# New places for the convolution's steps, the evacuations and the token sums beside the output projection of a fused convolution and SwiGLU kernel

## The chip, the cores and the metric

The kernel runs on one core of one Trainium2 chip. The metric is the device time of one execution in microseconds (us). Each core has a matrix engine (TensorE, PE in the profile, with its weight loads listed apart as PEld), a vector engine (VectorE, DVE), an activation engine (ScalarE, ACT), a general engine (GpSimd, POOL) and a queue that issues most DMAs here (SyncE, SP). Every engine works through its own queue in the order in which the program issued the instructions to it. An instruction whose input is not ready holds up everything behind it on that engine.

## The reference

`x` is 8 x 4096 x 192 in fp32. A causal depthwise convolution with seven taps comes first; each of eight heads of 24 channels has its own softmax-normalised taps. Its output is read as 32768 tokens of 192 channels. Each token is RMS-normalised and goes through a SwiGLU layer without bias.

```python
xn = x / rms * rms_g
g = xn @ w_gate                       # 192 -> 1536
silu = g * (1.0 / (1.0 + np.exp(-g)))
val = xn @ w_val                      # 192 -> 1536
return (silu * val @ w_out)           # 1536 -> 192
```

Everything is computed in fp32.

## The kernel before

**Tiling.** The tokens are cut into 32 pairs (`PAIRS`) of two tiles of 512 tokens. The gate half of the 192 to 1536 product lies in partitions 0 to 63 (`h = 0`), the value half in partitions 64 to 127 (`h = 1`). TensorE works on both halves beside each other. The `h = 1` stream runs `LAG = 138` planned units behind `h = 0`.

**A pair has two stages on TensorE.** In the first, four units (`NU`, function `unit`) each make three of the twelve 128-column blocks of the gate and the value product for both tiles. A bilinear scheme uses 15 matrix products where 18 would be needed, so sums of PSUM banks follow on the other engines; they are listed in `PLAN` (line 88). A code letter names the engine (`T` TensorE, `A` ScalarE, `V` VectorE, `G` GpSimd), a second the act (`P` product, `S` and `F` copies, `R` and `D` sums, `G` silu, `M` the gating multiply). The plan of a unit spans 1509 units but its last entries lie behind that, up to 1912: the last unit's tail falls into the second stage. In it are, on VectorE, four entries at 31, 102, 174 and 245 units after the second stage's start, on ScalarE two silus at 62 and 200, and on GpSimd three multiplies at 82, 243 and 403.

In the second stage (`outer`) TensorE multiplies the gated blocks by `w_out`: for two tiles `g` and four groups `j` of 128 tokens, twelve matmuls of 192 columns for each half. The two halves are sums over different parts of the contraction and are added when they leave PSUM: `low` (line 607) copies the `h = 0` bank by ScalarE, `upp` (line 611) adds the `h = 1` bank by VectorE, and `store` sends the tile out through SP.

**PSUM banks.** Each half has four banks (`free`, line 448). Tile `g = 0` uses all four, one for each `j`. Tile `g = 1` puts two `j` into one bank and so needs two banks; the first is the one that `low` and `upp` of `g = 0, j = 0` give back. The matmul that takes it is number `n = 48` of its half.

**What runs beside `outer`.** The convolution of the pair after next (`conv(p + 2, 1)`): tap 0 is eight `tensor_scalar` on VectorE (line 340, called the first tap below), taps 1 to 6 are eight multiplies each on ScalarE (line 355) and one addition of 128 x 1536 on VectorE (line 359). A multiply's result lies in one of three buffers (`prods`). The last step of `conv` issues the load of a later pair's `x` on SP. Then `norm(p + 2)`: eight squares with sums on ScalarE (line 371), two small instructions on GpSimd, eight scalings, half on ScalarE and half on VectorE. Further `fetch(p + 1)`, the four DMAs that bring the next pair's transposed tokens into `xb`, and `x_sums(p + 1)`: eleven sums of 128 x 512 on VectorE (line 441), which the bilinear scheme's products read in the next pair.

**Order.** Nothing is scheduled at run time. Every instruction, or every step of a generator between two `yield`s, is put on one list with a due time in planned units (`put`, `later`), and `emit` issues the list in the order of those times. The due time thus sets only the order in each engine's queue. For `outer`, `STEP` is 37.5 units a matmul, `OUT` is 3600 units for the stage, and `OVER` is how long after the last matmul of a group its evacuation is put. `base` in the code below is the start of `outer`.

Of the kernel before, what the change touches and what calls it, by code (L numbers as in the profile page):

```python
# [18 lines left out]
def kernel(  # L19
# [14 lines left out]
    H, K = weight.shape  # L34
# [31 lines left out]
    XSUM = (  # L66
        (0, 1, 4), (1, 2, 6), (2, 0, 6), (9, 3, 5), (3, 3, 8), (4, 7, 15), (5, 4, 15), (6, 5, 7),
        (7, 0, 1), (8, 1, 2), (9, 8, 15),
    )
# [71 lines left out]
    def load(p):  # L141

        if p >= PAIRS:
            return
        b, t0 = p // NB, (p % NB) * PT
        t = x_sb[p] = xs.tile([P, NJ + HALO, D], F32, name="x_sb")
        first = 0
        if t0 == 0:


            nc.vector.memset(t[0:1, 0:HALO, :], 0.0)
            nc.sync.dma_start(
                out=t[0:1, HALO:, :], in_=x[b, 0:NJ, :].rearrange("(o r) d -> o r d", o=1)
            )
            parts = ((1, 16), (16, P))
        else:
            parts = ((0, P),)
        for lo, hi in parts:
            row = x[b, t0 + lo * NJ - HALO, :]
            src = bass.AP(  # L160
                tensor=row.tensor, offset=row.offset,
                ap=[[NJ * D, hi - lo], [D, NJ + HALO], [1, D]],
            )
            nc.sync.dma_start(out=t[lo:hi, :, :], in_=src)
# [161 lines left out]
    def conv(p, alone=0):  # L326


        if p >= PAIRS:
            return  # L330
        t = x_sb.pop(p)
        y = ys[p] = work.tile([P, NJ, D], F32, name="y")
        for k in range(K):
            xk = t[:, k : k + NJ, :]
            if k < alone:
                for h in range(H):
                    hs = slice(h * GS, (h + 1) * GS)
                    w = taps[:, h, k : k + 1]
                    if k == 0:
                        nc.vector.tensor_scalar(  # L340
                            out=y[:, :, hs], in0=xk[:, :, hs], scalar1=w, scalar2=None,
                            op0=ALU.mult,
                        )
                    else:
                        nc.vector.scalar_tensor_tensor(
                            out=y[:, :, hs], in0=xk[:, :, hs], scalar=w, in1=y[:, :, hs],
                            op0=ALU.mult, op1=ALU.add,
                        )
                    if h % 4 == 3:
                        yield  # L350
                continue
            m = y if k == 0 else prods.tile([P, NJ, D], F32, name="m")
            for h in range(H):
                hs = slice(h * GS, (h + 1) * GS)
                nc.scalar.mul(m[:, :, hs], xk[:, :, hs], taps[:, h, k : k + 1])  # L355
                if h % 2:
                    yield
            if k > 0:
                nc.vector.tensor_tensor(out=y[:], in0=y[:], in1=m[:], op=ALU.add)  # L359
            yield  # L360
        load(p + 1)

    def norm(p, fast=False, share=False):
        if p >= PAIRS:
            return
        y = ys[p]
        ss = work.tile([P, NJ], F32, name="ss")
        sq = work.tile([P, D], F32, name="sq")
        na = NJ // 2 if fast else NJ
        for j in range(na):  # L370
            nc.scalar.activation(  # L371
                out=sq[:], in_=y[:, j, :], func=AF.Square, accum_out=ss[:, j : j + 1]
            )
            if j % 2:
                yield
        if fast:
            s2 = prods.tile([P, NJ, D], F32, name="m")
            nc.vector.tensor_tensor(
                out=s2[:, na:, :], in0=y[:, na:, :], in1=y[:, na:, :], op=ALU.mult
            )  # L380
            nc.vector.tensor_reduce(out=ss[:, na:], in_=s2[:, na:, :], axis=AX.X, op=ALU.add)
        r = work.tile([P, NJ], F32, name="r")
        nc.gpsimd.tensor_scalar(  # L383
            out=r[:], in0=ss[:], scalar1=1.0 / D, scalar2=1e-6, op0=ALU.mult, op1=ALU.add
        )
        nc.gpsimd.tensor_tensor(out=r[:], in0=r[:], in1=nhalf[:], op=ALU.pow)
        yield
        for j in range(NJ):
            if (fast or share) and j % 2:
                nc.vector.tensor_scalar(  # L390
                    out=y[:, j, :], in0=y[:, j, :], scalar1=r[:, j : j + 1],
                    scalar2=None, op0=ALU.mult,
                )
            else:
                nc.scalar.mul(y[:, j, :], y[:, j, :], r[:, j : j + 1])
            if j % 2:
                yield

    def place(p):

        if p >= PAIRS:
            return
        y = ys.pop(p)
        nt = work.tile([P, D // Q, Q, NJ], F32, name="nt")
        yv = y[:].rearrange("p j (c a) -> p c j a", a=Q)
        nv = nt[:].rearrange("p c b j -> p c j b")
        for c in range(D // Q):  # L410
            nc.vector.transpose(out=nv[:, c], in_=yv[:, c])
            yield
        xd = scr[p] = dram.tile([D, PT], F32, name="xd")
        to = xd[:].rearrange("(c a) (q t) -> q a c t", a=Q, q=NQ)
        for q in range(NQ):
            nc.sync.dma_start(
                out=to[q], in_=nt[q * Q : (q + 1) * Q].rearrange("p c b j -> p c (b j)")
            )
        yield

    def x_op(i):
        return xb[:, i // KP, i % KP, :] if i < 2 * KP else xc[:, i - 2 * KP, :]
# [13 lines left out]
    def x_sums(p):  # L436
        if p >= PAIRS:
            return

        for d, a, b in XSUM:  # L440
            nc.vector.tensor_tensor(out=xc[:, d, :], in0=x_op(a), in1=x_op(b), op=ALU.add)  # L441
            yield
# [18 lines left out]
    def put(at, do):  # L461
        heapq.heappush(line, (at, next(tick), do))

    def emit(until):
        while line and line[0][0] < until:
            heapq.heappop(line)[2]()
# [108 lines left out]

    STEP = 100 * D / T
    OUT = 2 * (T // P) * FC * STEP
    OVER = 120

    def outer(p, hts, base):  # L580

# [48 lines left out]
        def evac(dst, bks, w):  # L630
            put(base + n * STEP + OVER, functools.partial(low, dst, bks, w))
            put(base + n * STEP + LAG + OVER, functools.partial(upp, dst, bks, w))

        for g in range(2):
# [9 lines left out]
            else:  # L644
                for j in range(0, 4, 2):
# [3 lines left out]
                    evac(o_sb[:, j : j + 2, :].rearrange("p j d -> p (j d)"), b, 2 * D)  # L649
            put(base + n * STEP + LAG + OVER + 1, functools.partial(store, g, o_sb))  # L650

# [67 lines left out]
    def later(it, *places):  # L719
        for at in places:  # L720
            put(at, functools.partial(next, it, None))
# [3 lines left out]
    for p in range(PAIRS):  # L725
        base = p * PAIR
        if p > 0:
            hts = []
            pl = place(p + 1)
            for u in range(NU):  # L730
                at = base + u * SPAN
                put(at - 1, lambda u=u, hts=hts, at=at: hts.append(unit(u, at)))
                later(pl, *[at + i for i in ROOM])
        base += NU * SPAN

        def begin(p=p, hts=hts, base=base):
            outer(p, hts, base)

        put(base - 1, begin)
        put(base + LAG, functools.partial(fetch, p + 1))  # L740
        if p == 0:
            later(ws, *range(int(base), int(base) + 600, 100))
        cv = conv(p + 2, 1)
        later(cv, base + 40, base + 100, *[base + 290 + 66 * i for i in range(15)],
              *[base + 1390 + 66 * i for i in range(16)])
        later(norm(p + 2, share=True), *[base + 2400 + 128 * i for i in range(4)],
              *[base + 2920 + 90 * i for i in range(6)])
        later(x_sums(p + 1), *[base + 1680 + 150 * i for i in range(len(XSUM) + 1)])
        emit(base + OUT)
    emit(float("inf"))  # L750
# [28 lines left out]
```

## Time and profile before

| what | value |
|---|---|
| median of 3 runs | 2859.8 us (2857.16 to 2860.85) |
| the profiled execution's own time | 2857.99 us |
| its span, first to last instruction | 2856.2 us |
| mean granted TensorE clock | 0.989 |
| PE busy | 2734.8 us, 96% |
| PEld busy | 1872.4 us, 66% |
| DVE busy | 2282.2 us, 80% |
| ACT busy | 2199.9 us, 77% |
| POOL busy | 1206.7 us, 42% |

Shares are averages over both stages of all pairs. The prediction looks into single pairs. It uses the list of waits, the chain of waits that ended last, timelines of one engine, and tables of windows; each is explained where it is quoted. All times in those views are microseconds from the span's start.

### The profile page before, as it was taken

The numbers are of one execution on the slowest core, as the hardware profiler recorded it, in microseconds if no ns is written. First come the engines' busy times: TensorE is split into PE (matmuls) and PEld (weight loads), VectorE is DVE, ScalarE is ACT, GpSimd is POOL, SyncE is SP. The second block draws the span as 40 slices with busy tenths as digits, with TensorE's granted clock in tenths as the row PEclk, the third lists the DMA queues.
The fourth block names the chain that finished last, engine by engine and source line by source line (L and its number), as shares of the span: only waits on it lengthen the run. The fifth ranks groups of instructions, "written<-read, shape, count | busy, mean of one in ns | idle before, by whom it ended". The sixth has DMA issues, their size and how long they took to land.

```text
span 2856.2 us, 53815 instructions
## 1 busy us (share of the span) xinstructions
PE 2734.8 (96%) x20144; PEld 1872.4 (66%) x20144; DVE 2282.2 (80%) x3631; ACT 2199.9 (77%) x5013; POOL 1206.7 (42%) x1033
## 2 busy tenths in 40 slices
PE   3999999999999999999999999999999999999999
PEld 1576776666676667766667766677666677666776
DVE  7788878887778888788887888887888878888864
ACT  6678778877778787788777787877887777878754
POOL 1854334443334543344433345433444333454333
PEclk9999999999999999999999999999999999999999
DMA  6221222112121211221121212112211222121110
GB/s 155 70 64 43 53 65 59 39 44 63 53 65 39 59 44 53 65 59 40 42 64 54 65 39 59 43 54 64 59 40 42 65 54 64 39 60 43 34 45 12
DMA packets 95606, 155.24 MB, mean 54 GB/s; under 512 B 6896, under 2 KB 64752, under 8 KB 91256
## 3 DMA queue, kind: packets, MB, share of 16 engines
q1 hardware_dynamic: 94272, 150.20, 20.7%
q8 instruction: 158, 2.59, 0.4%
q0 software_dynamic: 512, 1.57, 0.2%
q14 instruction: 104, 0.85, 0.1%
q10 hardware_dynamic: 560, 0.03, 0.0%
HBM read 101.44 MB, written 50.33 MB: 53 GB/s over the span
## 4 chain that ended last, share of the span: by engine, by line
PE 75%; ACT 12%; DVE 8%; issue 3%; POOL 0%; DMA 0%; DVEq 0%; SPq 0%; POOLq 0%
PE ps L508 53%; PE ps L587 20%; ACT m L355 11%; DVE y L340 3%; DVE tile L530 2%; PE ps L558 1%; DVE ht L530 1%; DVE xc L441 1%; DVE ps L519 1%; ACT tile L534 0%; DVE o_sb L611 0%; POOL wf L301 0%; ACT o_sb L607 0%; DMA xb<-xd 0%; PE ps L598 0%
## 5 line engine op out<-in xcount | busy, mean ns | idle before, releaser
L508 PE MATMUL ps<-xc,wf 64*128 64x512 f32 x4960 | 1540.5, 593 | 0.0
L587 PE MATMUL ps<-wo_sb,ht 64*128 64x192 f32 x12288 | 1103.6, 329 | 65.3 <-DVE o_sb L611 52.2
L587 PEld LDWEIGHTS ps<-wo_sb,ht 64*128 64x128 f32 x12288 | 1082.9, 191 | 96.8 <-DVE o_sb L611 60.8
L508 PEld LDWEIGHTS ps<-xc,wf 64*128 64x128 f32 x4960 | 697.0, 187 | 559.1 <-issue 413.8
L537 POOL TENSOR_TENSOR ht<-ht,tile 128x512 f32<-128x512 f32 x620 | 773.7, 1272 | 651.0 <-ACT tile L534 551.0
L508 PE MATMUL ps<-xb,wf 64*128 64x512 f32 x2480 | 1038.4, 589 | 0.0
L517 ACT ACTIVATE tile<-ps 128x512 f32<-128x512 f32 x1488 | 820.1, 597 | 166.2 <-PE ps L508 136.4
L508 PEld LDWEIGHTS ps<-xb,wf 64*128 64x128 f32 x2480 | 419.2, 187 | 233.3 <-issue 202.4
L355 ACT ACTIVATE m<-x_sb,taps 128x192 f32<-128x192 f32 x1520 | 543.2, 444 | 7.0 <-DMA x_sb<-in_x_dram 6.3
L534 ACT ACTIVATE tile<-tile 128x512 f32<-128x512 f32 x620 | 374.8, 625 | 128.0 <-DVE tile L530 124.2
L359 DVE TENSOR_TENSOR y<-y,m 128x1536 f32<-128x1536 f32 x190 | 334.9, 1763 | 166.6 <-ACT m L355 166.0
L530 DVE TENSOR_TENSOR tile<-ps,tile 128x512 f32<-128x512 f32 x620 | 411.6, 680 | 0.0
L525 POOL TENSOR_TENSOR tile<-tile,tile 128x512 f32<-128x512 f32 x248 | 310.4, 1274 | 233.0 <-DVE tile L521 233.0
L530 DVE TENSOR_TENSOR ht<-ps,tile 128x512 f32<-128x512 f32 x620 | 401.3, 680 | 0.0
L383 POOL TENSOR_SCALAR r<-ss 128x8 f32<-128x8 f32 x32 | 6.6, 207 | 690.6 <-ACT sq L371 663.5
L530 DVE TENSOR_TENSOR ps<-ps,tile 128x512 f32<-128x512 f32 x248 | 173.5, 699 | 148.3 <-PE ps L508 146.4
L517 ACT ACTIVATE ps<-ps 128x512 f32<-128x512 f32 x372 | 216.2, 581 | 46.8 <-PE ps L508 32.1
L611 DVE TENSOR_TENSOR o_sb<-ps,o_sb 128x192 f32<-128x192 f32 (+1 forms) x192 | 78.1, 420 | 178.6 <-PE ps L508 94.2
L521 DVE COPY tile<-ps 128x512 f32<-128x512 f32 x248 | 170.1, 686 | 5.9 <-PE ps L508 5.8
L371 ACT ACTIVATE sq<-y 128x192 f32<-128x192 f32 x252 | 91.5, 363 | 102.4 <-DVE y L359 95.5
L519 DVE TENSOR_SCALAR ps<-ps 128x512 f32<-128x512 f32 x248 | 164.2, 695 | 0.0
L607 ACT COPY o_sb<-ps 128x192 f32<-128x192 f32 (+1 forms) x192 | 68.7, 358 | 111.3 <-PE ps L587 111.3
(54 smaller groups left out, 1206.1 us busy)
## 6 DMA issues: line engine op xcount, KB each, us to landing
xb<-xd SPq DMA_DIRECT2D x128, 384.0 KB, 6.3
x_sb<-in_x_dram SPq DMA_DIRECT2D x24, 1344.0 KB, 6.5
xd<-nt SPq DMA_DIRECT2D x128, 192.0 KB, 3.4
out_dram<-o_sb SPq DMA_DIRECT2D x64, 384.0 KB, 2.8
x_sb<-in_x_dram SPq DMA_DIRECT2D x8, 1176.0 KB, 9.4
ht<-in_moe_w_gate_dram SPq DMA_DIRECT2D x12, 192.0 KB, 9.0
ht<-in_moe_w_val_dram SPq DMA_DIRECT2D x12, 192.0 KB, 7.3
o_sb<-in_moe_w_out_dram POOLq DMA_DIRECT2D x8, 192.0 KB, 2.8
```

The source lines that it names most:

```text
L355: nc.scalar.mul(m[:, :, hs], xk[:, :, hs], taps[:, h, k : k + 1])
L359: nc.vector.tensor_tensor(out=y[:], in0=y[:], in1=m[:], op=ALU.add)
L371: nc.scalar.activation(out=sq[:], in_=y[:, j, :], func=AF.Square, accum_out=ss[:, j : j + 1])
L508: nc.tensor.matmul(out=new(v, h, True) if first else old(v, h), lhsT=wf[u][HALF[h], WAT[i], :], rhs=x_op(XOP[i])[HALF[h]], start=first, st ...
L517: nc.scalar.activation(out=dst, in_=src, func=AF.Copy, scale=float(s))
L519: e.tensor_scalar(out=dst, in0=src, scalar1=-1.0, scalar2=None, op0=ALU.mult)
L521: e.tensor_copy(out=dst, in_=src)
L525: e.tensor_tensor(out=grab((v, h)), in0=a, in1=b, op=plus(s))
L530: e.tensor_tensor(out=dst, in0=src, in1=t, op=plus(s))
L534: nc.scalar.activation(out=dst, in_=src, func=AF.Silu)
L537: e.tensor_tensor(out=hv(v), in0=src, in1=tl["g", v][:], op=ALU.mult)
L587: nc.tensor.matmul(out=bank(h, bks[h])[:, w : w + D], lhsT=hts[f // NF][HALF[h], g, f % NF, j * P : (j + 1) * P], rhs=wo_sb[HALF[h], f, :] ...
```

## The change

`OVER` goes from 120 to 50: all evacuations, and the stores behind them, are put 70 units earlier.

The first tap's two steps of four instructions move from 40 and 100 units after the start of `outer` to 250 and 255, behind the last unit's four VectorE entries (31, 102, 174, 245).

The ScalarE multiplies of tap 1 to 6 start at 280, 612, 944, 1276, 1668 and 2000, two every 83 units, with the VectorE addition 332 units after each start. Before, they came two every 66 units from 290 on, with a gap from 1214 to 1390, and the additions were at 554, 884, 1214, 1654, 1984 and 2314. The `x` load's issue goes from 2380 to 2340.

`norm`: the four steps of squares go from 2400, 2528, 2656, 2784 to 2560, 2688, 2816, 2944; the GpSimd step from 2920 to 3070; the four steps of scalings from 3010, 3100, 3190, 3280 to 3340, 3380, 3420, 3460.

`x_sums`: before, one every 150 units from 1680 to 3180. Now at 1690, 2020, 2060, and then one every 70 units from 2345 to 2835.

No instruction is added, removed or changed in its operands. `PLAN` is untouched.

```diff
-    OVER = 120
+    OVER = 50
...
-        cv = conv(p + 2, 1)
-        later(cv, base + 40, base + 100, *[base + 290 + 66 * i for i in range(15)],
-              *[base + 1390 + 66 * i for i in range(16)])
-        later(norm(p + 2, share=True), *[base + 2400 + 128 * i for i in range(4)],
-              *[base + 2920 + 90 * i for i in range(6)])
-        later(x_sums(p + 1), *[base + 1680 + 150 * i for i in range(len(XSUM) + 1)])
+        starts = [280 + 332 * k + (60 if k > 3 else 0) for k in range(K - 1)]
+        later(conv(p + 2, 1), *[base + i for i in (250, 255)],
+              *[base + i + 83 * n for i in starts for n in range(5)], base + 2340)
+        later(norm(p + 2, share=True), *[base + 2560 + 128 * i for i in range(4)],
+              base + 3070, *[base + 3340 + 40 * i for i in range(5)])
+        later(x_sums(p + 1), *[base + i for i in (1690, 2020, 2060)],
+              *[base + 2345 + 70 * i for i in range(len(XSUM) - 2)])
```

## The prediction

> **What bounds the kernel now.** First, what TensorE waits for. In the list of waits, restricted to TensorE, a row is: the waiting line, who released it, us in total, times, longest.
>
> ```profile
> PE ps L587 <- DVE o_sb L611: 52.2, 29, 1.8
> PE ps L587 <- ACT o_sb L607: 13.0, 29, 0.7
> ```
>
> Both wait 29 times, once a pair in 29 of the 32, on an evacuation of `outer`. Second, the chain of waits: start, length, what. The rows are like pieces of several pairs.
>
> ```profile
> 154.78 48.31 PE ps L508 x223
> ...
> 2336.84 48.31 PE ps L508 x216
> ...
> 2407.08 11.11 PE ps L587 x133
> 2423.17 48.31 PE ps L508 x216
> ...
> 2511.17 48.31 PE ps L508 x216
> ...
> 2581.41 12.79 PE ps L587 x133
> 2599.18 48.31 PE ps L508 x216
> ...
> 2669.42 11.11 PE ps L587 x133
> 2685.51 50.52 PE ps L508 x226
> ...
> 2768.74 50.52 PE ps L508 x226
> ```
>
> From the first product stage shown to the one at 2599.18 there are 28 pairs in 2444.40 us, 87.30 us each. There are two kinds: 2423.17 - 2336.84 = 86.33 us, with 133 matmuls in 11.11 us, and 2511.17 - 2423.17 = 88.00, where a like piece (2581.41) takes 12.79. The last pair shown takes 2768.74 - 2685.51 = 83.23 us: it has no convolution beside `outer` and no such wait. So **a pair without the waits is 83.23 us**, the short kind loses 3.10, the long kind 4.77. The two idle gaps in the list of waits come to only 65.2/29 = 2.25 a pair, because the other half's stream is still draining when one half stops.
>
> Third, windows of 3 to 36 us: the stretch, its length, busy time of PE, PEld, DVE, ACT, POOL (with counts), granted clock, DMA share, GB/s. The first is `outer` of the first pair, the second that of a pair of the long kind, the third and fourth the stall in it and the part after.
>
> ```profile
> 122.00:153.30 31.30, 31.30 (x382) 31.30 (x381) 23.43 (x35) 23.68 (x74) 17.06 (x23) 1.00 0.28 83
> 640.16:676.30 36.14, 33.90 (x385) 33.31 (x383) 26.05 (x39) 24.61 (x77) 5.64 (x5) 0.95 0.35 94
> 656.40:659.80 3.40, 1.56 (x14) 1.27 (x14) 2.44 (x3) 3.40 (x13) 0.00 (x0) 1.00 0.00 0
> 661.04:664.45 3.41, 3.41 (x26) 3.41 (x24) 3.41 (x6) 2.46 (x8) 0.00 (x0) 0.50 0.02 5
> ```
>
> In the long kind the clock stands at 0.50 for 3.41 us right after the stall, and half of that, 1.7 us, is the 1.67 us between the kinds. In the first pair TensorE is busy for the whole 31.30 us, though that pair has all of the convolution beside it.
>
> **Why the evacuation is late.** Timelines around one `outer`, TensorE, then VectorE, then ScalarE: start, length, engine, line, count, idle time before it and who ended it. A row of several instructions spans them all.
>
> ```profile
> 640.16 0.32 PE L587 MATMUL ps<-wo_sb,ht 64*128 64x192 f32 x1
> 656.68 1.56 PE L587 MATMUL ps<-wo_sb,ht 64*128 64x192 f32 x14 [0.44 <-ACT o_sb L607]
> 660.04 0.43 PE L587 MATMUL ps<-wo_sb,ht 64*128 64x192 f32 x2 [1.80 <-DVE o_sb L611]
> ...
> 641.14 3.66 DVE L340 TENSOR_SCALAR y<-x_sb,taps 128x192 f32<-128x192 f32 x8
> 657.36 1.76 DVE L359 TENSOR_TENSOR y<-y,m 128x1536 f32<-128x1536 f32 x1 [1.22 <-ACT m L355]
> 659.04 0.68 DVE L441 TENSOR_TENSOR xc<-xb 128x512 f32<-128x512 f32 x1
> 659.64 0.35 DVE L611 TENSOR_TENSOR o_sb<-ps,o_sb 128x192 f32<-128x192 f32 x1
> ...
> 645.43 0.63 ACT L534 ACTIVATE tile<-tile 128x512 f32<-128x512 f32 x1 [4.23 <-DVE tile L530]
> 645.97 10.46 ACT L355 ACTIVATE m<-x_sb,taps 128x192 f32<-128x192 f32 x30
> ```
>
> Call the stage's start b, here 640.16. The first tap goes first on VectorE (641.14). The last unit's sum stands behind it, so ScalarE's last silu waits 4.23 us and starts at b + 5.27; the multiplies queued behind it start at b + 5.81. Thirty of them end at 656.43, and only then comes `low`, which releases TensorE's first stall. VectorE's fourth addition waits for two more multiplies, one token sum follows, and `upp` runs at 659.64 (b + 19.48); TensorE goes on at 660.04. One cause lies behind both stalls: 3.6 us of lateness handed from VectorE to ScalarE and back.
>
> **The sums ahead of the first tap.** The trace has this order already, in the last pairs, where the first tap is missing. TensorE, VectorE, ScalarE:
>
> ```profile
> 2735.86 0.32 PE L587 MATMUL ps<-wo_sb,ht 64*128 64x192 f32 x1
> ...
> 2736.84 0.68 DVE L530 TENSOR_TENSOR tile<-ps,tile 128x512 f32<-128x512 f32 x1
> 2738.04 0.68 DVE L530 TENSOR_TENSOR ht<-ps,tile 128x512 f32<-128x512 f32 x1
> ...
> 2737.56 0.63 ACT L534 ACTIVATE tile<-tile 128x512 f32<-128x512 f32 x1 [0.66 <-DVE tile L530]
> 2748.77 0.32 ACT L607 COPY o_sb<-ps 128x192 f32<-128x192 f32 x1 [10.58 <-PE ps L587]
> ```
>
> The sum starts at b + 0.98, the silu at b + 1.70. The multiplies follow a silu by 645.97 - 645.43 = 0.54, so at **b + 2.24 instead of 5.81**. Thirty take 10.46: b + 12.70. In the last row `low` waits for nothing but TensorE, and starts at b + 12.91. So ScalarE is there 0.2 us early and `low` runs when the matmuls allow it. One silu, at b + 1.70, is the only ScalarE work that gains from VectorE directly; all the rest is the queue moving up.
>
> **The first tap behind them** starts 0.60 (half of the distance 2738.04 - 2736.84, two sums) after the last sum, at b + 2.78. What it takes there no row shows. Its median row, its neighbour on GpSimd in the pair above, and the rows of the first pair, which has b = 121.94:
>
> ```profile
> L340 DVE TENSOR_SCALAR y<-x_sb,taps x248: 303/308/1327, 11.0 to 2653.9; 128x192 f32<-128x192 f32 x124
> ...
> 640.79 2.52 POOL L537 TENSOR_TENSOR ht<-ht,tile 128x512 f32<-128x512 f32 x2 [1.11 <-ACT tile L534]
> ...
> 121.94 0.65 PE L587 MATMUL ps<-wo_sb,ht 64*128 64x192 f32 x3
> 134.86 0.32 ACT L607 COPY o_sb<-ps 128x192 f32<-128x192 f32 x1 [1.76 <-PE ps L587]
> 135.91 1.76 DVE L359 TENSOR_TENSOR y<-y,m 128x1536 f32<-128x1536 f32 x1 [3.09 <-ACT m L355]
> 138.29 0.34 DVE L611 TENSOR_TENSOR o_sb<-ps,o_sb 128x192 f32<-128x192 f32 x1
> 145.20 0.36 ACT L371 ACTIVATE sq<-y 128x192 f32<-128x192 f32 x1 [3.13 <-DVE y L359]
> 151.13 1.49 ACT L395 ACTIVATE y<-y,r 128x192 f32<-128x192 f32 x4 [1.70 <-POOL r L386]
> ```
>
> At the median 308 ns, eight take at most 2.5 us; here they took 3.66, beside two multiplies of 1.26 each on GpSimd. In the new place a third such multiply comes up beside them. I bound the step by 2.5 and 3.66 + 1.26 = 4.92, and take 3.66, the same instructions beside the same engine. Even at 4.92 it ends at b + 7.70. Three additions, 1.68 from start to start (659.04 - 657.36), then start at 7.70, 9.38 and 11.06; the third also needs 24 multiplies, b + 2.24 + 24 x 0.349 = 10.61. The fourth tap's multiplies reuse the first one's buffer from 10.61 on, and the first addition ends at 7.70 + 1.76 = 9.46. So VectorE is free at b + 12.74 at the latest. [...]
>
> **Evacuations 70 units earlier, multiplies and additions to match.** In the new order ScalarE has `low` (1512.5) ahead of the fourth tap's last two multiplies (1525); VectorE has the fourth addition (1608), then `upp` (1650.5), and the first token sum (1690) behind it instead of ahead. In the first pair, `low` was followed by the same two multiplies, and the fourth addition started 135.91 - 134.86 = 1.05 after it. So here: `low` b + 12.91, addition b + 13.96, `upp` b + 15.64 to 15.98. That is the added head-of-line wait: ScalarE can now stand at `low` for TensorE (0.2 us), with multiplies behind it. When is `upp` too late? In the first pair it ended at 138.63, b + 16.69, and TensorE never idled. **So `upp` has at least 0.7 us to spare** where it was 3.1 us late against the same mark (659.99 - 640.16 = 19.83, less 16.69). `low` ran at b + 12.92 in that pair, as it will here. The other three pairs of evacuations stand between multiplies and additions as before, and the banks they free are wanted only 24 matmuls later.
>
> **Squares, scalings, token sums, the loads and stores.** They cost what they did. Ahead of the squares stand the sixth addition and, on ScalarE, the same multiplies and copies; in the first pair they started 145.20 - 134.86 = 10.34 after `low` and the scalings 5.93 after that. That gives b + 23.25, 29.18 and, with 1.49, an end at 30.67. What each must not hold up:
>
> ```profile
> 667.04 1.28 DVE L441 TENSOR_TENSOR xc<-xb,xc 128x512 f32<-128x512 f32 x2
> ...
> 2767.49 0.48 ACT L607 COPY o_sb<-ps 128x384 f32<-128x384 f32 x1 [7.55 <-PE ps L587]
> ```
>
> The last `low` is ready at 2767.49 - 2735.86 = b + 31.63, 1.0 later. The eight token sums behind the sixth addition take some 0.6 each (two in 1.28) and end at 23.25 + 8 x 0.6 = b + 28.1; the next products come after the 31.3 us of the first window. SP's queue keeps its order (fetch, store, load, store), each a little earlier, and none of its transfers appears in TensorE's waits after the start-up. I cost all of these at nothing; without the 1.0 us of cover each further us would cost 29, one in each pair.
>
> **The sum.** Nothing late is left on TensorE's side, so each of 29 pairs falls to 83.23 us. 28 pairs give 2444.40 - 28 x 83.23 = 113.96. The 29th (2669.42) is of the short kind, 3.10. Together **117.1 us**: 29 x 3.10 = 89.9 for the stalls, and 27.2, some 16 stretches of 1.67, for the clock. From the profiled execution's 2857.99 that leaves 2740.9. The median of the runs, 2859.8, stands 1.8 above that execution; I say **2742**.
>
> **The rivals.**
>
> *A short stall stays (0.09).* My chain has 0.7 us to spare at `upp` and rests on ScalarE reaching `low` at b + 12.70. If multiplies, port or buffers cost 0.9 us more than that, `upp` ends at b + 16.7, and each half us beyond costs 14.5: 2756 at half a us. For it: 0.2 us of room on ScalarE is thin. Against: every duration is from the same instructions.
>
> *The half clock stays (0.04).* Free of stalls, 16 stretches of 1.67 could remain: 2741 + 27 = 2768. [...] Against: neither the first pair nor the last two show a loss; at 16 in 29 by chance, three such pairs in a row have (13/29)^3, 9%. [...]
>
> *The change doesn't do what it says (0.02).* If the sums were late by their own inputs, not by the first tap, nothing moves: 2858. The row at 2736.84 speaks against it.
>
> *Slower (0.03).* The tail spills into the next pair: eight sums and the scalings now stand packed behind the sixth addition, and the scalings ahead of the last `low` and the next pair's bank copies. With over 1.0 us of delay there TensorE waits, at 29 us for each us; the gain is used up at 1.0 + 117.1/29 = 5.0, and at 6 the time is 2741 + 5 x 29 = 2886. For it: the squares are placed 160 units later than before. Against: in the first pair the squares had 3.13 us of idle ahead of them, so the additions set their time, not their place.
>
> **How the numbers follow.** The forecast has 0.82: all stalls go. It and the short stalls up to half a us make the range: 2736 (the runs before lie 2.6 below their median; three more for the bounds of the first tap and rounding) to 2757. A measurement of this kernel can tell about 0.2%, 5.7 us, from no change. Forecast, short stall and half clock are faster: 0.95; same 0.02; slower 0.03.
>
> **What would show it.** In the changed profile: TensorE's two waits on line 607 and 611 gone or under 0.2 us a pair; clock 1.000 but for the start-up; the silu about b + 1.7, multiplies b + 2.2, `low` b + 12.9 ended by TensorE, `upp` b + 15.6; pairs of 83.2 us throughout. I am wrong if `low` is still preceded by a multiply without idle time, if `upp` is behind b + 16.7, or if a wait on a token sum or a bank copy appears at the start of the product stage.

## The result and the profile after

The changed kernel takes 2741.43 us (median of 4 runs, 2740.69 to 2743.35), the kernel before 2860.1 us in the same comparison (median of 4, 2857.16 to 2860.85). The ratio is 0.9588, 95% interval 0.9571 to 0.9605. The forecast was 2742 us, within 2736 to 2757.

First, the chain of work that ended last, by engine, on the page of the kernel before and then of the changed kernel:

```profile
PE 75%; ACT 12%; DVE 8%; issue 3%; POOL 0%; DMA 0%; DVEq 0%; SPq 0%; POOLq 0%
```

```profile
PE 97%; POOL 1%; DVE 0%; DMA 0%; issue 0%; ACT 0%; SPq 0%; POOLq 0%; DVEq 0%
```

TensorE's own work is now nearly the whole chain; ScalarE and VectorE had 20% of it before.

The list of what TensorE waited for, changed kernel, whole (us in total, times, longest):

```profile
PE ps L558 <- DMA xb<-xd: 45.0, 1, 45.0
PE ps L558 <- ACT tile L564: 3.5, 1, 3.5
PE ps L558 <- DVE wf L271: 2.1, 1, 2.1
PE ps L558 <- DVE ht L565: 0.3, 1, 0.3
```

All four are at line 558, the first pair's products at the start-up. The waits on lines 607 and 611 are gone. A window over one `outer` of the changed kernel (length, then busy time of PE, PEld, DVE, ACT, POOL, clock, DMA share, GB/s):

```profile
621.49:652.90 31.41, 31.41 (x386) 31.41 (x384) 25.45 (x39) 24.67 (x76) 6.04 (x5) 1.00 0.41 109
```

TensorE is busy for all of 31.41 us. In the kernel before, the pair shown needed 36.14 us for the same matmuls. The timeline of this pair, TensorE, VectorE, ScalarE, answers to the rows that the prediction showed; its b is 621.49:

```profile
621.49 0.65 PE L587 MATMUL ps<-wo_sb,ht 64*128 64x192 f32 x3
...
622.38 0.68 DVE L530 TENSOR_TENSOR tile<-ps,tile 128x512 f32<-128x512 f32 x1
...
624.17 3.09 DVE L340 TENSOR_SCALAR y<-x_sb,taps 128x192 f32<-128x192 f32 x8
...
635.41 1.76 DVE L359 TENSOR_TENSOR y<-y,m 128x1536 f32<-128x1536 f32 x1 [1.61 <-ACT m L355]
637.09 0.35 DVE L611 TENSOR_TENSOR o_sb<-ps,o_sb 128x192 f32<-128x192 f32 x1
...
623.09 0.63 ACT L534 ACTIVATE tile<-tile 128x512 f32<-128x512 f32 x1 [0.67 <-DVE tile L530]
623.62 10.46 ACT L355 ACTIVATE m<-x_sb,taps 128x192 f32<-128x192 f32 x30
634.36 0.32 ACT L607 COPY o_sb<-ps 128x192 f32<-128x192 f32 x1 [0.28 <-PE ps L587]
...
643.62 0.36 ACT L371 ACTIVATE sq<-y 128x192 f32<-128x192 f32 x1 [1.93 <-DVE y L359]
...
650.22 1.49 ACT L395 ACTIVATE y<-y,r 128x192 f32<-128x192 f32 x4 [2.50 <-POOL r L386]
653.11 0.48 ACT L607 COPY o_sb<-ps 128x384 f32<-128x384 f32 x1 [1.39 <-PE ps L587]
```

The sum comes at b + 0.89, the silu at 1.60, the multiplies at 2.13, `low` at 12.87, ended by TensorE, the fourth addition at 13.92, `upp` at 15.60. Both `low` rows now end their idle time on TensorE: ScalarE waits for the matmuls and not the other way round.

Counted from the trace's matmul records, `outer` (first matmul to the first product of the next pair) takes 31.42 us in every one of the 31 pairs that have a next one. Before, it took 31.42 in the first and in the last of these, about 34.5 in 13 and about 36.2 in 16. The product stage takes 51.81 us in both, with a few that are up to 0.16 us longer.

### The profile page after: what moved, and what is told of

The parts are those of the page before. It is cut to its first block, busy times and chain, and to the rows that moved or that the text cites. A ratio compares the mean times of both kernels' runs of the same rounds, so it can differ in the third digit from the quotient of the medians.

```text
span 2739.5 us, 53838 instructions
## 1 busy us (share of the span) xinstructions
PE 2684.4 (98%) x20144; PEld 2168.9 (79%) x20144; DVE 2277.5 (83%) x3631; ACT 2206.7 (81%) x5013; POOL 1226.2 (45%) x1033
## 4 chain that ended last, share of the span: by engine, by line
PE 97%; POOL 1%; DVE 0%; DMA 0%; issue 0%; ACT 0%; SPq 0%; POOLq 0%; DVEq 0%
PE ps L508 58%; PE ps L587 37%; PE ps L558 2%; PE ps L598 0%; POOL wf L301 0%; DMA xb<-xd 0%; DMA xd<-nt 0%; DVE nt L411 0%; DVE wf L271 0%; ACT y L395 0%; DVE ht L565 0%; POOL o_sb L205 0%; POOL r L386 0%; DVE y L359 0%; POOL wf L297 0%
## 5 line engine op out<-in xcount | busy, mean ns | idle before, releaser
L508 PE MATMUL ps<-xc,wf 64*128 64x512 f32 x4960 | 1510.4, 593 | 0.0
L508 PEld LDWEIGHTS ps<-xc,wf 64*128 64x128 f32 x4960 | 808.6, 187 | 314.2 <-ACT ps L517 40.4
L587 PE MATMUL ps<-wo_sb,ht 64*128 64x192 f32 x12288 | 1048.1, 323 | 0.0
L587 PEld LDWEIGHTS ps<-wo_sb,ht 64*128 64x128 f32 x12288 | 1044.4, 187 | 0.8 <-issue 0.4
L508 PE MATMUL ps<-xb,wf 64*128 64x512 f32 x2480 | 1008.2, 589 | 0.0
L508 PEld LDWEIGHTS ps<-xb,wf 64*128 64x128 f32 x2480 | 444.8, 187 | 161.8 <-DVE ps L519 0.9
L525 POOL TENSOR_TENSOR tile<-tile,tile 128x512 f32<-128x512 f32 x248 | 310.7, 1276 | 212.7 <-DVE tile L521 212.7
L383 POOL TENSOR_SCALAR r<-ss 128x8 f32<-128x8 f32 x32 | 28.1, 879 | 677.7 <-ACT sq L371 650.8
```

What stands on the lines that cost most here:

```text
L508: nc.tensor.matmul(out=new(v, h, True) if first else old(v, h), lhsT=wf[u][HALF[h], WAT[i], :], rhs=x_op(XOP[i])[HALF[h]], start=first, st ...
L525: e.tensor_tensor(out=grab((v, h)), in0=a, in1=b, op=plus(s))
L587: nc.tensor.matmul(out=bank(h, bks[h])[:, w : w + D], lhsT=hts[f // NF][HALF[h], g, f % NF, j * P : (j + 1) * P], rhs=wo_sb[HALF[h], f, :] ...
```

## The experiments

Four questions: which part of the change does it, what the tap's lateness is made of, how much lateness there is room for, and what becomes of a lateness that is not removed. Each time is the median of 4 executions. `outer` and "product stage" in the table are the typical lengths from the matmul records.

| run | us (median) | ratio to before, 95% | `outer` | product stage |
|---|---|---|---|---|
| first tap only | 2741.85 | 0.9583 (0.9567 to 0.9599) | 31.42 | 51.81 |
| evacuations only | 2796.77 | 0.9776 (0.9761 to 0.9790) | 31.68 | 53.45 |
| all but the first tap | 2822.87 | 0.9870 (0.9855 to 0.9884) | 33.92, in 7 pairs 35.5 to 35.9 | 51.81 |
| spacing only | 2846.59 | 0.9950 (0.9935 to 0.9965) | 34.3 or 36.0 | 51.81 |
| first tap twice | 2741.56 | 0.9583 (0.9568 to 0.9597) | 31.42 | 51.81 |
| first tap three times | 2826.34 | 0.9882 (0.9868 to 0.9897) | 33.85, in 6 pairs 35.4 to 35.9 | 51.81 |
| first tap four times | 2962.69 | 1.0361 (1.0346 to 1.0377) | 38.1 or 39.2 | 51.81 |
| no GpSimd beside the tap, in the kernel before | 2780.15 | 0.9723 (0.9708 to 0.9737) | 32.78 | 51.81 |
| evacuations only, scalings left out | 2797.00 | 0.9782 (0.9766 to 0.9798) | 31.68 | 53.45 |
| evacuations and token sums | 2763.43 | 0.9660 (0.9644 to 0.9676) | 31.64 | 52.12, in every fourth or so 52.98 |

### The first tap alone

```diff
-        later(cv, base + 40, base + 100, *[base + 290 + 66 * i for i in range(15)],
+        later(cv, base + 250, base + 255, *[base + 290 + 66 * i for i in range(15)],
```

> The kernel before with the first tap alone moved behind the last unit's sums; evacuations, multiplies, scalings and token sums stay at their old places. Theory (the first tap ahead of the sums is the one cause of the lateness): silu at b + 1.7, low at b + 12.9, upp behind one token sum at b + 16.2 to 16.6, just inside the latest time that the first pair showed (16.69), so no stall and 2741 us. Rival (the evacuations' and token sums' new places are needed too): upp comes up to some tenths of a us too late in each of 29 pairs, 2745 to 2760 us.

Measured: 2741.85 us (2740.97 to 2742.28), the same as the whole change. The new places of the tap's two steps give everything; the new evacuations, spacing, scalings and token sums add nothing that shows once the tap stands behind the sums. `upp` still runs behind a token sum there, 2.27 us after the fourth addition starts and not 1.68, and that is in time:

```profile
636.62 1.76 DVE L359 TENSOR_TENSOR y<-y,m 128x1536 f32<-128x1536 f32 x1 [1.60 <-ACT m L355]
638.89 0.35 DVE L611 TENSOR_TENSOR o_sb<-ps,o_sb 128x192 f32<-128x192 f32 x1
```

(Timeline of VectorE, first tap only.)

### The evacuations alone

```diff
-    OVER = 120
+    OVER = 50
```

> The kernel before with OVER = 50 alone; the first tap stays ahead of the sums. Theory in its strict form (nothing helps but the tap's place): still two stalls, 2840 to 2860 us. What the queue orders say instead: ScalarE has low now behind 28 multiplies and not 30, so it starts at b + 5.81 + 28 x 0.349 = b + 15.6 and ends some 0.3 us after TensorE wants the bank; VectorE has upp ahead of the fourth addition and not behind it, so it ends at b + 16.3, in time. That is 2741 + 29 x 0.3 = 2750 us, without half clock, and would mean that the evacuations' places alone are worth nine tenths of the gain.

Measured: 2796.77 us, neither. In `outer` the queue orders were right: only 0.26 us of loss a pair is left (31.68 against 31.42), and no stretch of half clock (mean granted clock 0.998, as in the changed kernel). So the strict form of the theory falls: `low` behind 28 multiplies and `upp` ahead of the fourth addition do nearly without the tap's move. But 1.64 us a pair came up at a place that the expectation had not looked at, the start of the product stage: 29 x (0.26 + 1.64) = 55 us over 2741. TensorE's list of waits and ScalarE's timeline of this run:

```profile
PE ps L508 <- ACT o_sb L607: 41.0, 29, 1.4
```

```profile
656.78 0.36 ACT L371 ACTIVATE sq<-y 128x192 f32<-128x192 f32 x1 [2.80 <-DVE y L359]
...
662.93 1.49 ACT L395 ACTIVATE y<-y,r 128x192 f32<-128x192 f32 x4 [2.05 <-POOL r L386]
664.33 0.46 ACT L607 COPY o_sb<-ps 128x384 f32<-128x384 f32 x1
664.69 0.59 ACT L517 ACTIVATE tile<-ps 128x512 f32<-128x512 f32 x1
```

```profile
664.00 0.68 DVE L441 TENSOR_TENSOR xc<-xc 128x512 f32<-128x512 f32 x1
```

The lateness was not removed; the first evacuations only no longer stand behind it. It travels on, through the additions, squares and scalings, to the end of the stage. The list names the last `low`, behind the scalings; the last row, VectorE's last token sum, ends within 0.2 us of it. The next run tests the name.

### The evacuations alone, ScalarE's scalings left out

```diff
-            else:
+            elif not share:
                 nc.scalar.mul(y[:, j, :], y[:, j, :], r[:, j : j + 1])
```

> The kernel before with OVER = 50, and ScalarE's four scalings of line 395 left out in all pairs that share them with VectorE, so half of the tokens stay unscaled there. With OVER = 50 alone the stalls in outer were down to 0.25 us a pair and TensorE lost 1.64 us a pair at the start of the product stage, waiting on the last low. Theory (the tail spills: that low stands behind four scalings that wait for GpSimd): without them the loss at the product stage goes, 2742 + 29 x 0.25 = 2749 us. Rival (the last low is late for another reason, its matmuls or the squares ahead of it): 2797 us as with OVER = 50 alone.

Measured: 2797.00 us, the rival's number, though not by the rival's reason. The last `low` is in time now (it waits for TensorE), and TensorE waits for just as long; the list names something else. The list of waits, then ScalarE's and VectorE's timelines of this run:

```profile
PE ps L508 <- DVE xc L441: 41.0, 29, 1.4
```

```profile
662.74 0.48 ACT L607 COPY o_sb<-ps 128x384 f32<-128x384 f32 x1 [1.71 <-PE ps L587]
...
663.08 0.32 DVE L390 TENSOR_SCALAR y<-y,r 128x192 f32<-128x192 f32 x1 [2.31 <-POOL r L386]
663.31 0.69 DVE L441 TENSOR_TENSOR xc<-xb 128x512 f32<-128x512 f32 x1
663.92 0.31 DVE L390 TENSOR_SCALAR y<-y,r 128x192 f32<-128x192 f32 x1
664.14 0.68 DVE L441 TENSOR_TENSOR xc<-xc 128x512 f32<-128x512 f32 x1
```

The last two token sums stand between VectorE's scalings, which wait for GpSimd's two small instructions, and the second product of the next pair reads the last sum. With OVER = 50 alone the last `low` and the last token sum ended within 0.2 us of each other, and the list of waits named only the later one. Taking the lateness from the one that is named changed the name and not the time.

### The evacuations and the token sums

```diff
-    OVER = 120
+    OVER = 50
...
-        later(x_sums(p + 1), *[base + 1680 + 150 * i for i in range(len(XSUM) + 1)])
+        later(x_sums(p + 1), *[base + i for i in (1690, 2020, 2060)],
+              *[base + 2345 + 70 * i for i in range(len(XSUM) - 2)])
```

> The kernel before with OVER = 50 and the token sums at their new places; the first tap stays ahead of the last unit's sums, multiplies and scalings stay where they were. With OVER = 50 alone TensorE lost 1.64 us a pair at the start of the product stage; leaving out ScalarE's scalings did not change that, it only gave the wait another name, the token sums. Theory (the last token sums stand behind VectorE's scalings, which wait for GpSimd): with the sums ahead of the scalings that loss goes and 0.25 us a pair in outer stays, 2749 us; up to 2760 if ScalarE's copies behind the late scalings then come too late for the products after them. Rival (ScalarE's last low and its copies were the wait after all): 2785 to 2797 us.

Measured: 2763.43 us, 3 over the upper end of the theory and far from the rival. With the sums ahead of the scalings, 1.33 of the 1.64 us a pair go. The last `low` still stands behind the scalings, yet TensorE starts the second product before it (TensorE's and ScalarE's timelines of this run):

```profile
657.33 0.59 PE L508 MATMUL ps<-xc,wf 64*128 64x512 f32 x1
...
658.25 0.46 ACT L607 COPY o_sb<-ps 128x384 f32<-128x384 f32 x1
```

So that product does not need this `low`. With `OVER` = 50 alone the list of waits had named a late instruction that held up nothing there; the token sum did. What stays is 0.31 us, and 1.17 in 7 of the 29 pairs. For the 7 the list of waits names ScalarE's copies of the banks, which come behind the late `low`; no run tests that name:

```profile
PE ps L508 <- ACT tile L517: 4.8, 7, 0.7
```

So the token sums' new place is worth something, 33 us (2796.77 - 2763.43), as long as the stage runs late. With the tap behind the sums nothing runs late, and it is worth nothing.

### All but the first tap, and the spacing alone

The changed kernel with the tap back in front; the second of the two also with the old `OVER`.

```diff
-        later(conv(p + 2, 1), *[base + i for i in (250, 255)],
+        later(conv(p + 2, 1), *[base + i for i in (40, 100)],
```

> The changed kernel with the first tap back at 40 and 100, ahead of the last unit's sums. Theory: ScalarE is 3.6 us late again, low at b + 16.2 behind 30 multiplies, upp behind the fourth addition at b + 18.9, so stalls of 0.44 and about 1.2 us on TensorE's row; 29 x (3.10 - 0.6) = 72 us above the changed kernel, 2813 us, if stretches of half clock need more idle time in one window than that; 2841 us if as many of them stay. Rival (the evacuations and the spacing do it without the tap): 2741 to 2750 us.

> The changed kernel with the first tap back at 40 and 100 and OVER = 120: of the change there is only the spacing of multiplies, additions, scalings and token sums. Theory: low now stands behind 32 multiplies (b + 17.0), the fourth addition follows at once, a token sum comes between, upp at b + 19.3: the end of the stall is 0.15 us earlier than before, 29 x 0.15 = 4 us, 2854 us with the same half clock and 2828 without it, since the idle time is cut in two more even parts (about 1.2 and 0.9 us). Rival (measured spacing pays by itself): under 2800 us.

Measured: 2822.87 and 2846.59 us. Both go with the theory, both between its two ends, since the half clock came back in some pairs: 7 of 29 in the first, 13 in the second (mean granted clock 0.994 and 0.990). With the tap in front, `outer` lost 33.92 - 31.42 = 2.50 and some 2.9 us a pair. TensorE's waits in the first:

```profile
PE ps L587 <- DVE o_sb L611: 34.8, 29, 1.2
PE ps L587 <- ACT o_sb L607: 13.4, 29, 0.7
```

The longer gap is 1.20 us a pair, as expected, and the shorter is what it was. The evacuations at 50 gain far less here than alone (2846.59 - 2822.87 = 24 us, against 2861.07 - 2796.77 = 64), because the new spacing has 30 multiplies ahead of `low` and the fourth addition ahead of `upp` again.

### No GpSimd beside the first tap

In the kernel before, two of GpSimd's multiplies in the tail of the last unit are left out, results 5 and 2.

```diff
-                e.tensor_tensor(out=hv(v), in0=src, in1=tl["g", v][:], op=ALU.mult)
+                if not (eng == "G" and u == NU - 1 and v in (2, 5)):
+                    e.tensor_tensor(out=hv(v), in0=src, in1=tl["g", v][:], op=ALU.mult)
```

> The kernel before, with two of GpSimd's three multiplies in the last unit's tail left out (results 5 and 2 of the fourth unit are not multiplied by the silu); they are what ran beside the first tap, whose first two instructions took 1.04 and 1.32 us and not 0.31. Theory (GpSimd holds up VectorE's first tap, and that is half of the lateness): the tap takes 1.9 and not 3.6 us, the sums, the silu and all multiplies come 1.8 us earlier, low at b + 14.4 in time, upp at b + 17.7 to 18.0, one stall of 1.1 us a pair, no half clock: 2773 us. Rival (the first two are slow by themselves, as the first of a row): 2858 us.

Measured: 2780.15 us, 7 over the theory, 78 under the rival. The tap's group in this run (duration in ns, least, median, most) and its row:

```profile
L340 DVE TENSOR_SCALAR y<-x_sb,taps x248: 306/314/510, 10.9 to 2575.1; 128x192 f32<-128x192 f32 x124
```

```profile
628.00 1.92 DVE L340 TENSOR_SCALAR y<-x_sb,taps 128x192 f32<-128x192 f32 x8
```

No instruction takes 1.04 or 1.32 us any more, and eight take 1.92 and not 3.66. One gap is left, and no half clock (mean granted clock 0.998):

```profile
PE ps L588 <- DVE o_sb L612: 31.4, 29, 1.1
```

TensorE's row is idle for 1.1 us a pair, as expected, but the stage is 1.36 us longer (32.78 against 31.42), and that makes the 7 us. The lateness of 3.6 us was thus half the tap's own work, 1.92 us, and half, 1.74, came with GpSimd's multiplies. In the kernel before, the instructions of 1.04 and 1.32 us (641.14 to 643.42) ran beside two of these (640.79 to 643.31), and the other six took some 0.31 each; without the two multiplies the longest of all took 0.51. By what path GpSimd holds VectorE up no run shows.

### The first tap twice, three and four times

In the changed kernel, each first-tap instruction is issued n times in a row; the same values are written again.

```diff
-                        nc.vector.tensor_scalar(
+                        for _ in range(n if alone == 1 else 1):
+                            nc.vector.tensor_scalar(
```

> The changed kernel with each of the eight first-tap instructions of line 340 issued three times in a row, for every pair whose first tap alone is on VectorE (the same values are written again). 16 more at 0.23 us, start to start, end the tap at b + 9.4 and not 5.8. Theory (the tap has cover behind the sums; only upp's time counts): additions at 9.5, 11.2, 12.9 and 14.6; the fourth tap's multiplies wait 0.8 us for their buffer, low at b + 13.4, upp at b + 16.3 to 16.6, still in time: 2741 us. Rival (VectorE's work itself is on the path now): 29 x 3.7 = 107 us more, 2848.

> The same with each first-tap instruction four times: 24 more. Theory: the tap ends at b + 11.3, additions at 11.4, 13.1, 14.7 and 16.4, upp at b + 18.1 to 18.5. TensorE wants the bank at about 1.3 + 48 x 0.325 = b + 16.9, so 1.6 us are lost in each of 29 pairs, 46 us: 2788, without half clock, since the idle time is under 1.45 us. So the eight instructions that cost nothing from twice to three times cost 46 us from three to four times.

Measured: 2826.34 and 2962.69 us, where 2741 and 2788 were expected. The price of a repeated instruction was wrong. VectorE's timeline, three times, with b = 636.15:

```profile
638.93 8.66 DVE L341 TENSOR_SCALAR y<-x_sb,taps 128x192 f32<-128x192 f32 x24
647.69 7.35 DVE L360 TENSOR_TENSOR y<-y,m 128x1536 f32<-128x1536 f32 x4
654.95 0.35 DVE L612 TENSOR_TENSOR o_sb<-ps,o_sb 128x192 f32<-128x192 f32 x1
```

ScalarE's timeline has the fourth tap's multiplies late, for a buffer that the first addition still reads:

```profile
649.48 2.19 ACT L356 ACTIVATE m<-x_sb,taps 128x192 f32<-128x192 f32 x6 [2.71 <-DVE y L360]
```

16 more took 8.66 - 3.09 = 5.6 us, 0.35 each: an instruction that writes where the one ahead of it wrote did not follow it at the 0.23 us of the others. (In the trace's records of this tap, single starts lie about 0.35 us apart ahead of a repeat, and 0.23 to 0.24 ahead of an instruction with a new output.) The tap ended at b + 11.4, the additions ran without a pause, and `upp` came at b + 18.8. That is a little behind the place where four times had been expected, with some 1.6 us of loss; it lost 2.4. Another run with the new price settles whether the mechanism stands:

> The changed kernel with each first-tap instruction issued twice. With three times each, a repeated instruction cost 0.35 us and not the 0.23 assumed, so the tap ended at b + 11.3 (the place that four times was expected to reach) and upp came at b + 18.7. Theory with that price (the tap has cover up to about 2.5 us): 8 x 0.35 = 2.8 us more, tap ends at b + 8.6, additions at 8.7, 10.4, 12.1 and, waiting for the multiplies as ever, 13.9; upp at b + 15.6: 2741 us. Rival (any lateness of the tap goes through to TensorE): three times cost 85 us for 5.6 us more a pair, so 2.8 us would cost about 42, 2784.

```profile
624.52 5.82 DVE L341 TENSOR_SCALAR y<-x_sb,taps 128x192 f32<-128x192 f32 x16
637.70 0.35 DVE L612 TENSOR_TENSOR o_sb<-ps,o_sb 128x192 f32<-128x192 f32 x1
```

Measured: 2741.56 us. With b = 621.84 the tap ends at b + 8.5 and `upp` starts at b + 15.9, 0.3 later than in the changed kernel, and nothing of the 2.7 us reaches the time. The next 2.8 us cost 85, the 2.8 after them 136. So there is cover, and it lies between 2.7 and 5.6 us. Behind it the loss grew faster than the tap. The clock's record has half clock in 6 pairs with three times and in all 30 with four (mean granted clock 0.995 and 0.962), where none had been expected. The 1.45 us under which four times was to stay free of it was the author's estimate, and no run shows such a bound; the nearest measured are the single gaps of 1.41 us of the evacuations alone, 29 times without half clock. TensorE's waits, three times and then four times (two rows):

```profile
PE ps L588 <- DVE o_sb L612: 56.5, 30, 2.2
```

```profile
PE ps L588 <- ACT o_sb L608: 76.8, 30, 2.8
PE ps L588 <- DVE o_sb L612: 33.1, 30, 1.9
```

With four times `low` is late too, behind the multiplies that wait for a buffer. The idle time grew by (76.8 + 33.1 - 56.5)/30 = 1.8 us a pair, less than the tap's 2.8; the rest of the 136 us comes together with the half clock, and how it divides no run shows.

## Why the prediction was right

**The cause.** "One cause lies behind both stalls: 3.6 us of lateness handed from VectorE to ScalarE and back." Shown: the tap's two steps alone give 2741.85 us, the rest without them 2822.87.

**The chain.** Forecast and measured, from b: silu 1.70 and 1.60, multiplies 2.24 and 2.13, `low` 12.91 and 12.87, fourth addition 13.96 and 13.92, `upp` 15.64 and 15.60. Each was taken from a pair of the old trace that already had that part of the new order, the last pairs for the sums and the first pair for the evacuations.

**The first tap.** Bounded by 2.5 and 4.92, taken as 3.66, measured 3.09. Of GpSimd's three multiplies only the last, which ended at 625.76, still ran well into it, and one instruction of the tap took over 1 us (1.32), not two. So the third multiply did not add to the price as the upper bound allowed for. Its end at b + 5.8 was far from the 8.5 that the run with two of each still hides.

**The tail.** Squares 23.25 and 22.13, scalings 29.18 and 28.73, last `low` 31.63 and 31.62. The cover forecast at 1.0 us was 1.39, the idle time ahead of the last `low`.

**The sum.** 117.1 us forecast; between the spans of the two profiled executions, 2856.2 and 2739.5, lie 116.7. All 29 pairs fell to the length of the last pair. The clock's record has half clock in 16 of the old stages, as the sum had it, and in none of the new ones.

**The rivals.** A short stall: none stayed; in the first-tap run `upp` had one token sum more ahead of it and was still in time. (That rival counts a port among what could cost more; no run shows one. Shown are one instruction of 1.32 us beside GpSimd and 3.09 us for the whole tap.) The half clock without a stall: none of the 31 stages in the profile after has it, and in the kernel before each of the 16 stretches came in the window after a stall of 1.80 us. Sums late by their own inputs: the sum now starts at b + 0.89. The rival on the slower side, the tail that spills into the next pair, did not happen in the changed kernel. As a mechanism it is real: it took 48 us (29 x 1.64) in the run with the evacuations alone, where the lateness had not been removed. The prediction put its gate at the scalings ahead of the last `low`; in that run the gate was the token sums behind VectorE's scalings, and the last `low` was late beside them without holding up that product.

**What the prediction did not say.** It costed the evacuations, the spacing and the token sums at nothing for harm, but left open what they gain. Beside the moved tap they gain nothing. Nor did it see that `OVER` alone would clear most of the stall in `outer` on the old tap's place.

## What to carry to other kernels

Where engines work through fixed queues, follow a stall back to the first instruction that runs late without being needed soon; here, moving that one made four other adjustments worthless. An earlier consumer without an earlier producer only passes the lateness on, to the end of the stage. And when two late things end together, the list of waits names the later one, which need not be the one that holds; a cause is found only when the time itself moves.

## What the runs showed of the hardware

**Half clock after a stall.** From 97 us to the last pair, all changes of the granted clock in the kernel before lie within 0.01 us of one grid of 3.41 us. Windows of the kernel before on that grid, a long pair's stall, then a short pair's and what follows:

```profile
657.62:661.04 3.42, 1.62 (x18) 1.33 (x17) 3.42 (x7) 3.42 (x12) 0.00 (x0) 1.00 0.00 0
...
746.37:749.78 3.41, 1.73 (x21) 1.73 (x22) 3.41 (x8) 3.41 (x12) 0.00 (x0) 1.00 0.00 0
749.78:753.20 3.42, 3.42 (x47) 3.42 (x45) 3.42 (x5) 1.72 (x5) 0.00 (x0) 1.00 0.18 57
```

TensorE was busy for 1.62 us of the first, and the next, from 661.04, ran at half clock (the prediction shows its row); it was busy for 1.73 of the second, and the one after it ran at full clock. Of the 29 gaps of 1.80 us, the 16 that lay whole in one window, over 0.2 us from its start, were followed by half clock; the 9 that an edge cut and the 4 that began in its first 0.13 us were not. A single gap of 1.41 us (evacuations alone) never was, 29 times, 18 of them whole in one window. Gaps of 0.44 and 1.20 us (all but the first tap) were, in 7 pairs where at least 1.55 us of the two fell into one window. So the stalls' place on the grid told the two kinds of pairs apart, in all 29, and in one run 1.55 us of idle time in a window of 3.41 were enough. No single bound fits the runs: 1.55 us sufficed in one and 1.68 did not in another, and with the first tap three times 1.87 us did not, in three windows where the gap began in the first 0.07 us.

**Two prices.** In the first tap repeated three times, a `tensor_scalar` that rewrote its predecessor's output cost 0.35 us and not 0.23 from start to start. GpSimd's small instruction of line 383 took a median of 0.196 us before and 0.647 after; in its new place it runs beside token sums on VectorE in all 30 pairs that have it beside `outer`; before, it ran beside no VectorE instruction in any of them. The scalings wait for GpSimd there, but the 1.39 us of cover ahead of the last `low` stayed.
